# Operands made in two parts between reordered blocks, and right-hand pools moved by 384 bytes

## The chip, the cores and the metric

The kernel runs on one core of a Trainium2 chip. What counts is the time of one execution in device microseconds (us): 597.5 us is the median of three runs of the kernel before.

## The reference

Three stages follow each other on 1152 rows (two batches of 576) of width 512. An attention with random features gives x. A first mixture of experts (MoE 1) sends each row to one of eight experts. A second one (MoE 2) puts every row through all of four experts and adds up the results with weights:

```python
def _moe2_ref(x, domain_probs, w1, w2):
    p = domain_probs / (domain_probs.sum(-1, keepdims=True) + 1e-09)
    out = np.zeros((N, D))
    for e in range(E):                       # 4 experts, D = 512, F = 1024
        h = np.maximum(x @ w1[e], 0.0)
        out += p[:, e:e + 1] * (h @ w2[e])
    return out
```

## The kernel before

Every product is made of three fp32r matmuls (high times high, high times low, low times high; lines 745 to 747). So each operand exists as a pair, a high part that ScalarE casts (line 104) and a low part that VectorE or GpSimd subtracts (line 105); the helper `split` does both.

**MoE 1** works on four chunks of 288 rows, held as columns. For a chunk, `unit1` makes the hidden layer (96 matmuls into `ph`), and `unit2` makes the output in four blocks d = 0 to 3 of 128 features (24 matmuls each into `py`). `add_yt` then multiplies a block by the gate (`yt`, line 826) and adds it to `x2T` (line 828), which has four rows of blocks, [128, 4, 1152]. Chunk c takes the columns 256c to 256c+255 and 32 of the columns above 1024.

**MoE 2** multiplies with a Winograd scheme: seven products instead of eight, of 2x2 blocks. Its columns come in two groups, `GROUPS = ((0, 320), (640, 256))`; group 1 is columns 640 to 1151. `x_side(g)` makes the seven x operands of a group out of `x2T`: high and low parts of the two halves into `xh` and `xl`, a part into `xd`, four sums and differences in place (lines 1111 to 1114), and splits of the results into `xh`, `xl` and, in `rest()`, into `xc`. Group 0 needs chunks 0 to 2, so `x_side(0)` stands ahead of `unit2(3)`. Group 1 needs chunk 3 as well, so `x_side(1)` stands in the main loop, behind the second first-layer step.

The main loop takes two slices (e, j) of the experts' hidden features at a time, an even j (i = 0) and an odd j (i = 1). `layer1(w1, g)` makes seven products `pp` of six matmuls of 320 or 256 columns, in a ring of five PSUM banks that VectorE and ScalarE empty. `layer2` makes a `po` of 512 columns for each of five (g = 0) or four (g = 1) tiles, six matmuls each, in a ring of three PSUM banks; VectorE adds each to `oa` or `ob` (line 1211 for the first slice, line 1213 later). Below, (0,0) is the even slice with group 0, (0,1) the even slice with group 1, and so on. In the first pair the order of the first layers is (0,0), (1,0), (0,1), (1,1); a second layer follows the next first layer.

The order on each engine is made when the program is built: instructions are put in order by their place in the program and by when the scheduler reckons their operands ready; at run time each engine's queue is strictly in order. So `x_side(1)` lies on VectorE between the evictions of the first two `layer1`.

**Addresses.** `w2` of the even slices lies in the pool `w2s0` on the right-hand side of SBUF, that of the odd slices in `w2s1` on the left. The right-hand pools are stacked from the top: `even` (a pad of 32 bytes a partition), `own`, which `xq` (`xd`) replaces later, `xr0` (`xc` of group 0) and `w2s0`. In the program as built before, the four tiles of `w2s0` begin at 201664, 203712, 205760 and 207808, those of `w2s1` at 155200, 157248, 159296 and 161344. Every tile on the left that TensorE reads in the loops here begins 64 bytes past a multiple of 512, those on the right 448 past one. A chunk's columns in `xh` begin 1152 bytes after those of the chunk before. The weights that TensorE loads (`w1` in the first layers, `hh` and `hl` in `layer2`) are all on the left.

Of the kernel before, what the change touches and what calls it, by code (L numbers as in the profile page):

```python
# [9 lines left out]
F32 = mybir.dt.float32  # L10
# [3 lines left out]
ALU = mybir.AluOpType  # L14
# [11 lines left out]
NC = 288  # L26
# [3 lines left out]
GROUPS = ((0, 320), (640, 256))  # L30
# [8 lines left out]
def moe_stack(ctx, tc, q, k, v, omega, w_gate, w_ogate, mw1, mw2, dprobs, dw1, dw2, out):  # L39
    nc = tc.nc  # L40
    TT, STT, TS = nc.vector.tensor_tensor, nc.vector.scalar_tensor_tensor, nc.vector.tensor_scalar

    def f32(ap):
        return ap.bitcast(F32)
# [58 lines left out]
    def split(hi, lo, src, eng=nc.vector, p=lambda i: i):  # L103
        p(nc.scalar.copy(hi, src))  # L104
        p(eng.tensor_tensor(lo, src, f32(hi), op=ALU.subtract))  # L105

    class Expert:
# [45 lines left out]
        def part(self, pool, tag, sink, shape, src, eng=None, p=lambda i: i):  # L153
            hi = pool.tile(shape, F32R, tag=tag + "h", name="whi")
            lo = pool.tile(shape, F32R, tag=tag + "l", name="wlo")
            split(hi, lo, src, eng or self.eng, p)
            sink.append((hi, lo))
# [9 lines left out]
    for c, w, pattern, base in ((0, 32, [[1, 32]], 0), (32, 32, [[1, 32]], 1), (64, 8, [[-1, 8]], 8),  # L167
                                (72, 32, [[0, 4], [1, 8]], 0), (104, 32, [[1, 4], [0, 8]], 0)):
        dst = i32[:, c:c + w]
# [398 lines left out]
    def sel_factors(c, b, eng, p=lambda i: i):  # L568
        t = cp.tile([128, 3, NE], F32, tag="selt", name="selt", bufs=2)
        bc = ohb[:, b:b + 1, :]  # L570
        p(eng.tensor_tensor(t[:, 0:2], g_all[:, 2 * c:2 * c + 2], bc.to_broadcast([128, 2, NE]), op=ALU.mult))
        p(eng.tensor_tensor(t[:, 2:3], grm[:, c:c + 1], bc, op=ALU.mult))

        def total():
            s = cp.tile([128, 3], F32, tag="sel", name="sel", bufs=2)
            p(nc.vector.tensor_reduce(s, t, axis=AX.X, op=ALU.add))
            return s
        return total

    def sel_static(c, b):  # L580
        return sel_factors(c, b, nc.vector)() if b else sel0[c]
# [9 lines left out]
    n = len(units)  # L591
# [19 lines left out]
    def dyn(w, e):  # L611
        return w[bass.ds(e, 1)].rearrange("o a b -> (o a) b")
# [11 lines left out]
    while st < n + 1 or to_turn or to_num or turned:  # L624
# [43 lines left out]
        if 0 <= st - 2 < n and units[st - 2][0] == "q":  # L668
            kind, b, hh, jp = units[st - 2]
# [18 lines left out]
        for x in ready:  # L688
            b, hh, u = x
# [53 lines left out]
    def mm3(ps, st_hl, mv_hl, start, stop):  # L743
        (sh_, sl_), (mh, ml) = st_hl, mv_hl
        nc.tensor.matmul(ps, sh_, mh, start=start, stop=False)  # L745
        nc.tensor.matmul(ps, sh_, ml, start=False, stop=False)  # L746
        nc.tensor.matmul(ps, sl_, mh, start=False, stop=stop)  # L747

    def l1(w1, xhc, xlc, *rings):
        hs = []  # L750
        for f in range(FB):
            pool, tag = rings[f % len(rings)]
            ps = pool.tile([128, NC], F32, tag=tag, name="ph")
            wh, wl = w1[f]
            for kb in range(KB):
                mm3(ps, (wh[:, kb, :], wl[:, kb, :]), (xhc[kb], xlc[kb]), kb == 0, kb == KB - 1)
            if f % 2 == 0:
                hh, hl = h_tiles(NC)
            hid(ps, hh[:, f % 2], hl[:, f % 2])
            hs.append((hh[:, f % 2], hl[:, f % 2]))  # L760
        return hs

    def l2_block(w2, hs, d, bank=None):
        pool, tag = bank or (ps_j, "pj")
        y = pool.tile([128, NC], F32, tag=tag, name="py")
        ds_ = slice(128 * d, 128 * d + 128)
        for f in range(FB):
            wh, wl = w2[f]
            mm3(y, (wh[:, ds_], wl[:, ds_]), hs[f], f == 0, f == FB - 1)
        return y  # L770

    def gate_row(s):

        dg = gp.tile([128, NC], F32, tag="dg", name="dg")
        for t in range(2):
            nc.scalar.activation(dg[:, 128 * t:128 * t + 128], ident, AF.Copy, scale=s[:, t:t + 1])
        nc.scalar.activation(dg[:, 256:NC], fold, AF.Copy, scale=s[:, 2:3])
        ps = nd2.tile([128, NC], F32, tag="nd", name="pg")
        nc.tensor.matmul(ps, ones, dg, start=True, stop=True)
        g = gp.tile([128, NC], F32, tag="gb", name="gb")  # L780
        nc.scalar.copy(g, ps)
        return g
# [3 lines left out]
    def unit1(c, w1, *rings):  # L786
        xhc = [xh[:, kb, NC * c:NC * c + NC] for kb in range(KB)]
        xlc = [xl[:, kb, NC * c:NC * c + NC] for kb in range(KB)]
        return l1(w1, xhc, xlc, *(rings or RINGS))

    def unit2_blocks(c, w2, hs, late=None):
        gb = gate_row(sel_static(c, c // 2))
        for d in range(KB):
            if d == KB - 1 and late is not None:
                late += [l2_block(w2, hs, d, (ps_k, "kv")), gb]
                yield
                return
            y = l2_block(w2, hs, d)
            for dst, src in zip(x2cols(c), (slice(0, 256), slice(256, NC))):
                TT(x2T[:, d, dst], y[:, src], gb[:, src], op=ALU.mult)  # L800
            yield

    def unit2(c, w2, hs):
        if c >= 2:
            gb = gate_row(sel_static(c, c // 2))
            return add_out(w2, hs, gb, list(zip(x2cols(c), (slice(0, 256), slice(256, NC)))))
        for _ in unit2_blocks(c, w2, hs):
            pass

    def x2cols(c):  # L810
        return slice(256 * c, 256 * c + 256), slice(1024 + 32 * c, 1056 + 32 * c)
# [8 lines left out]
    def add_out(w2, hs, gb, cols):  # L820
        for d in range(KB):
            add_yt(l2_block(w2, hs, d), gb, d, cols)

    def add_yt(y, gb, d, cols):
        yt = gp.tile([128, NC], F32, tag="yt", name="yt")
        TT(yt, y, gb, op=ALU.mult)
        for dst, src in cols:
            TT(x2T[:, d, dst], x2T[:, d, dst], yt[:, src], op=ALU.add)

    hs = unit1(0, E0.w1, (ps_j, "pj"), (ps_j, "pj"), (ps_j, "pj"), (ps_k, "kv"))  # L830
# [4 lines left out]
    pool_m = ExitStack()  # L835
    w2p = pool_m.enter_context(tc.tile_pool(name="w2p", bufs=8))
    gp = pool_m.enter_context(tc.tile_pool(name="gp", bufs=2))
    ctx.enter_context(tc.tile_pool(name="even", bufs=1, side="right")).tile([128, 8], F32, name="even")
    pool_o = ExitStack()
    own = pool_o.enter_context(tc.tile_pool(name="own", bufs=1, side="right")).tile([128, KB * 512], F32, name="own")  # L840
    pool_l = ExitStack()
# [1 line left out]
    x2T = yp.tile([128, KB, NX], F32, tag="y", name="x2T")  # L843
# [71 lines left out]
    hs = unit1(1, E0.w1)  # L915
# [57 lines left out]
    E1 = Expert(dyn(mw1, e), None, nc.vector)  # L973
# [48 lines left out]
    with tc.If(nx > 0, preferred_fallthrough_block=True, label="more"):  # L1022
        with tc.For_i(0, nx, 1) as it:
# [7 lines left out]
            hs = l1(E1.w1, xhc, xlc, *RINGS)  # L1031
            Expert(dyn(mw1, ln), None).load1(E1.w1)
            mi = mt[:, bass.ds(it, 1)].rearrange("p o c e -> p (o c) e")
            t = lp.tile([128, 4, 2, NE], F32, tag="xt", name="xt")
# [16 lines left out]
    hs = unit1(2, E1.w1)  # L1051
    unit2(2, E1.w2, hs)
    hs = unit1(3, E1.w1)
# [37 lines left out]
    def pair_of(pool, shape, tags):  # L1091
        return [pool.tile(shape, F32R, tag=t, name=t) for t in tags]

    xa = (xh, xl)
    xd = pair_of(xq, [128, 2, NX // 2], ("xdh", "xdl"))
    xops, xc = [], []

    def x_side(g, eng):
        base, n = GROUPS[g]
        a, b = x2T[:, :, base:base + n], x2T[:, :, base + n:base + 2 * n]  # L1100

        def part(dst, c, src, k=None):
            hi, lo = (t[:, :, c:c + n] for t in dst)
            if k is not None:
                hi, lo, src = (t[:, k:k + 2] for t in (hi, lo, src))
            split(hi, lo, src, eng)
            return [(hi[:, 2 * i:2 * i + 2], lo[:, 2 * i:2 * i + 2]) for i in range(src.shape[1] // 2)]

        b11, b21 = part(xa, base, a)
        b22, = part(xd, base // 2, b[:, 2:4])  # L1110
        eng.tensor_tensor(a[:, 0:2], b[:, 0:2], a[:, 0:2], op=ALU.subtract)
        eng.tensor_tensor(b[:, 0:2], b[:, 2:4], b[:, 0:2], op=ALU.subtract)
        eng.tensor_tensor(b[:, 2:4], b[:, 2:4], a[:, 0:2], op=ALU.subtract)
        eng.tensor_tensor(a[:, 2:4], b[:, 2:4], a[:, 2:4], op=ALU.subtract)
        t1, t4 = part(xa, base + n, a)

        def rest():
            t2, t3 = (part(xc[g], 0, b, i)[0] for i in (2, 0))
            xops.append((b11, b21, b22, t4, t1, t2, t3))

        return rest
# [19 lines left out]
    xc.append(pair_of(xr0, [128, KB, GROUPS[0][1]], ("xch", "xcl")))  # L1141
    x_side(0, nc.vector)()
    w2_ahead = [load_w2(0, 0)]
    unit2(3, E1.w2, hs)
    pool_m.close()
    w2s.append(ctx.enter_context(tc.tile_pool(name="w2s1", bufs=2)))
    xr1 = ctx.enter_context(tc.tile_pool(name="xr1", bufs=1))
# [76 lines left out]
    for p in range(0, 4 * NE2, 2):  # L1224
        ej = [divmod(p + i, 4) for i in range(2)]
        ws = {}
        for i, g in ((0, 0), (1, 0), (0, 1), (1, 1)) if p == 0 else ((0, 0), (0, 1), (1, 0), (1, 1)):
            e, j = ej[i]
            if i not in ws:
                ws[i] = ahead.pop(0) if ahead else load_pair(e, j), w2_ahead.pop() if w2_ahead else load_w2(e, j)  # L1230
            w1, w2 = ws[i]
            h = layer1(w1, g)
            if (p, i, g) == (0, 1, 0):
                x_side(1, nc.vector)()
            if late:
                layer2(*late)
            late = (e, j, g, h, w2)
# [30 lines left out]
```

## Time and profile before

| | |
|---|---|
| runs of the kernel before | 596.45, 597.5, 598.2 us |
| profiled execution: its own time | 597.24 us |
| span of its trace | 595.1 us |
| TensorE busy | 580.5 us (98%) |
| VectorE, ScalarE, GpSimd busy | 397.5, 256.1, 265.3 us |

The span runs from the first instruction to the last; what lies around it, 2.1 us, is start and end of the execution. Times in rows count from the start of the span. A busy TensorE is not one at its best speed: matmuls are pipelined, and a matmul that takes longer looks just as busy.

### The profile page before, as it was taken

Reading aid. Unit: us, or ns where it says so; the run is one execution under the profiler, and the core shown is the slowest. Engines: PE = TensorE matmul, PEld = TensorE weight load, DVE = VectorE, ACT = ScalarE, POOL = GpSimd, SP = SyncE. Lnnn points to the kernel's source line nnn. Section 1 sums busy time; section 2 is a strip of 40 time slices with the busy share of each in tenths; the row PEclk is TensorE's granted clock in tenths of the full one; section 3 lists DMA queues with packets and bytes.
Section 4 is the critical chain, followed back from the end, with each engine's and each line's share of the span. In section 5 each row is a group of like instructions: output and inputs, shape, how many; then the busy total and the mean of one; then the engine's idle time right before and its main releaser. Section 6 shows DMA issues by size and latency. Waiting matters only on the chain.

```text
span 595.1 us, 12003 instructions
## 1 busy us (share of the span) xinstructions
PE 580.5 (98%) x4674; PEld 523.1 (88%) x4675; DVE 397.5 (67%) x889; ACT 256.1 (43%) x625; POOL 265.3 (45%) x316
## 2 busy tenths in 40 slices
PE   9899999999999998999999999999999999999996
PEld 8778788997899997899888988998899889989995
DVE  6688777852667697656766676567566665676564
ACT  5888676023534253343424434334344244333230
POOL 6996085000010033757537456366375473663210
PEclk9999999999999998999999999999999999999999
DMA  7841262154540220022022022022003002200004
GB/s 184 218 124 47 80 208 80 52 215 151 206 145 1 71 72 1 1 72 72 0 72 72 1 72 72 1 72 72 1 20 104 20 1 72 73 0 1 1 0 159
DMA packets 42299, 42.86 MB, mean 72 GB/s; under 512 B 14848, under 2 KB 31488, under 8 KB 42240
## 3 DMA queue, kind: packets, MB, share of 16 engines
q1 hardware_dynamic: 41952, 42.00, 22.2%
q8 instruction: 38, 0.62, 0.4%
q14 instruction: 21, 0.17, 0.1%
q10 hardware_dynamic: 288, 0.07, 0.1%
HBM read 37.34 MB, written 4.72 MB: 71 GB/s over the span
## 4 chain that ended last, share of the span: by engine, by line
PE 67%; DVE 3%; DMA 1%; issue 1%; ACT 0%; SPq 0%; DVEq 0%
PE po L745 11%; PE po L746 11%; PE po L747 11%; PE pp L746 9%; PE pp L745 9%; PE pp L747 9%; PE py L745 1%; DMA st<-in_moe_w_dram 1%; PE py L747 1%; PE py L746 1%; PE ph L747 1%; PE ph L746 1%; PE ph L745 1%; DVE hl L736 1%; DVE c L1174 0%
## 5 line engine op out<-in xcount | busy, mean ns | idle before, releaser
L105 POOL TENSOR_TENSOR wlo<-st,whi 128x512 fp32r<-128x512 f32 x100 | 120.8, 1231 | 188.3 <-ACT whi L104 152.4
L104 ACT CAST whi<-st 128x512 fp32r<-128x512 f32 (+1 forms) x128 | 72.6, 596 | 142.6 <-PE po L747 50.0
L745 PE MATMUL po<-whi,hh 128*128 128x512 f32 x288 | 113.6, 394 | 1.9 <-DVE oa L1211 1.9
L747 PE MATMUL po<-whi,hl 128*128 128x512 f32 x288 | 113.5, 394 | 0.0
L746 PE MATMUL po<-wlo,hh 128*128 128x512 f32 x288 | 113.5, 394 | 0.0
L741 POOL TENSOR_TENSOR hl<-c,hh 128x320 fp32r<-128x320 f32 (+1 forms) x64 | 52.6, 823 | 88.0 <-ACT hh L740 72.3
L747 PE MATMUL pp<-xh,wlo 128*128 128x320 f32 (+1 forms) x256 | 75.8, 296 | 0.0
L746 PE MATMUL pp<-xl,whi 128*128 128x320 f32 (+1 forms) x256 | 75.8, 296 | 0.0
L745 PE MATMUL pp<-xh,whi 128*128 128x320 f32 (+1 forms) x256 | 75.8, 296 | 0.0
L1213 DVE SCALAR_TENSOR_TENSOR oa<-po,pb,oa 128x512 f32<-128x512 f32 x75 | 55.4, 748 | 30.0 <-PE po L747 30.0
L745 PEld LDWEIGHTS po<-whi,hh 128*128 128x128 f32 x288 | 54.3, 188 | 13.0 <-DVE oa L1211 2.1
L747 PEld LDWEIGHTS po<-whi,hl 128*128 128x128 f32 x288 | 54.4, 189 | 12.3
L746 PEld LDWEIGHTS po<-wlo,hh 128*128 128x128 f32 x288 | 54.4, 189 | 10.9
L1213 DVE SCALAR_TENSOR_TENSOR ob<-po,pb,ob 128x512 f32<-128x512 f32 x60 | 44.9, 749 | 28.3 <-PE po L747 28.3
L1174 DVE TENSOR_TENSOR c<-u,pp 128x320 f32<-128x320 f32 (+1 forms) x96 | 43.3, 452 | 22.1 <-PE pp L747 21.7
L739 ACT ACTIVATE c<-c 128x320 f32<-128x320 f32 (+1 forms) x64 | 28.5, 445 | 50.1 <-DVE c L1174 49.1
L745 PEld LDWEIGHTS pp<-xh,whi 128*128 128x128 f32 x256 | 48.6, 190 | 1.4
L746 PEld LDWEIGHTS pp<-xl,whi 128*128 128x128 f32 x256 | 48.6, 190 | 1.3
L747 PEld LDWEIGHTS pp<-xh,wlo 128*128 128x128 f32 x256 | 48.6, 190 | 0.0
L736 DVE SCALAR_TENSOR_TENSOR hl<-c,hh 128x320 fp32r<-128x320 f32 (+1 forms) x64 | 44.5, 729 | 0.2
L339 ACT ACTIVATE e<-pj,nb 128x128 f32<-128x128 f32 x144 | 39.6, 374 | 5.4 <-DVE nb L331 5.0
L745 PE MATMUL py<-hh,whi 128*128 128x288 f32 x128 | 39.3, 307 | 0.0
(263 smaller groups left out, 1272.2 us busy)
## 6 DMA issues: line engine op xcount, KB each, us to landing
st<-in_moe_w_dram SPq DMA_DIRECT2D x36, 512.0 KB, 4.5
st<-in_moe_w_dram SPq DMA_DIRECT2D x9, 1024.0 KB, 5.3
q<-in_q_dram SPq DMA_DIRECT2D x4, 512.0 KB, 5.1
v<-in_v_dram SPq DMA_DIRECT2D x16, 128.0 KB, 4.8
xs<-xn SPq DMA_DIRECT2D x16, 128.0 KB, 2.6
k<-in_k_dram SPq DMA_DIRECT2D x3, 512.0 KB, 4.9
out_dram<-oa SPq DMA_DIRECT2D x5, 256.0 KB, 2.0
own<-in_moe_w_dram SPq DMA_DIRECT2D x1, 1024.0 KB, 6.9
```

Of the source, the lines that this page charges most:

```text
L104: p(nc.scalar.copy(hi, src))
L105: p(eng.tensor_tensor(lo, src, f32(hi), op=ALU.subtract))
L339: pin(nc.scalar.activation(e[:, i], st_p[u][a][:, i], AF.Exp, bias=nb[:, i:i + 1]))
L736: STT(hl, src, 0.0, f32(hh), op0=ALU.max, op1=ALU.subtract)
L739: nc.scalar.activation(c, c, AF.Relu)
L741: nc.gpsimd.tensor_tensor(hl, c, f32(hh), op=ALU.subtract)
L745: nc.tensor.matmul(ps, sh_, mh, start=start, stop=False)
L746: nc.tensor.matmul(ps, sh_, ml, start=False, stop=False)
L747: nc.tensor.matmul(ps, sl_, mh, start=False, stop=stop)
L1174: TT(c, u, p, op=op)
L1213: STT(oacc[T], po, pc, oacc[T], op0=ALU.mult, op1=ALU.add)
```

## The change

It has three parts. The first block order of `unit2(3)` is written out: d = 0, 2, then `x_half(1, 0)`, then d = 1, 3, then `x_half(1, 1)`. Second, `x_half(g, k)` does the part of `x_side(1)` that reads and writes the block rows k and k + 2 of `x2T`; `x_rest` does what was `rest()`, at the place where `x_side(1)` stood. Third, the pad `even` grows from 32 to 416 bytes a partition, so that all right-hand pools lie 384 bytes lower.

```diff
-    ctx.enter_context(tc.tile_pool(name="even", bufs=1, side="right")).tile([128, 8], F32, name="even")
+    ctx.enter_context(tc.tile_pool(name="even", bufs=1, side="right")).tile([128, 104], F32, name="even")
...
+    def x_half(g, k, eng):
+        base, n = GROUPS[g]
+        def quarters(t, c):
+            return t[:, :, c:c + n].rearrange("p (h k) n -> p k h n", k=2)[:, k]
+        def part(dst, c, src):
+            split(*(quarters(t, c) for t in dst), src, eng)
+        a, b = quarters(x2T, base), quarters(x2T, base + n)
+        part(xa, base, a)
+        lo = slice(base // 2, base // 2 + n)
+        split(xd[0][:, k, lo], xd[1][:, k, lo], b[:, 1], eng)
+        eng.tensor_tensor(a[:, 0], b[:, 0], a[:, 0], op=ALU.subtract)
+        eng.tensor_tensor(b[:, 0], b[:, 1], b[:, 0], op=ALU.subtract)
+        eng.tensor_tensor(b[:, 1], b[:, 1], a[:, 0], op=ALU.subtract)
+        eng.tensor_tensor(a[:, 1], b[:, 1], a[:, 1], op=ALU.subtract)
+        part(xa, base + n, a)
+    def x_rest(g, eng):
+        base, n = GROUPS[g]
+        for i in (2, 0):
+            split(xc[g][0][:, i:i + 2], xc[g][1][:, i:i + 2], x2T[:, i:i + 2, base + n:base + 2 * n], eng)
...
-    unit2(3, E1.w2, hs)
+    gb = gate_row(sel_static(3, 1))
+    for k in range(2):
+        for d in (k, k + 2):
+            add_yt(l2_block(E1.w2, hs, d), gb, d, list(zip(x2cols(3), (slice(0, 256), slice(256, NC)))))
+        x_half(1, k, nc.vector)
     pool_m.close()
...
             if (p, i, g) == (0, 1, 0):
-                x_side(1, nc.vector)()
+                x_rest(1, nc.vector)
```

## Rows read from the trace of the kernel before

**Rows 1.** Waits of TensorE: us in total, times, longest us.
```profile
PE po L745 <- DVE oa L1211: 1.9, 1, 1.9
```

**Rows 2.** Windows: us, busy us of each engine, PEclk, DMA share, GB/s.
```profile
200.00:209.00 9.00, 9.00 (x70) 9.00 (x69) 3.75 (x11) 0.56 (x2) 0.00 (x0) 1.00 0.37 117
...
211.00:226.00 15.00, 15.00 (x95) 14.21 (x94) 15.00 (x25) 8.55 (x18) 5.60 (x6) 1.00 0.21 70
...
230.00:232.00 2.00, 2.00 (x6) 1.51 (x6) 0.75 (x1) 0.00 (x0) 0.00 (x0) 0.50 0.00 0
```

**Rows 3.** Timeline of TensorE, 221 to 234 us: start, us, instruction, [idle before].
```profile
221.23 0.39 PE L745 MATMUL po<-whi,hh 128*128 128x512 f32 x1
...
225.40 0.28 PE L745 MATMUL pp<-xh,whi 128*128 128x256 f32 x1
...
226.36 0.28 PE L747 MATMUL pp<-xh,wlo 128*128 128x256 f32 x1
228.55 0.50 PE L745 MATMUL po<-whi,hh 128*128 128x512 f32 x1 [1.92 <-DVE oa L1211]
...
229.82 0.52 PE L747 MATMUL po<-whi,hl 128*128 128x512 f32 x1
...
232.69 0.41 PE L745 MATMUL pp<-xh,whi 128*128 128x256 f32 x1
...
233.33 0.30 PE L745 MATMUL pp<-xch,whi 128*128 128x256 f32 x1
```

**Rows 4.** Timeline of VectorE, 209 to 230 us.
```profile
209.62 1.63 DVE L828 TENSOR_TENSOR x2T<-x2T,yt 128x256 f32<-128x256 f32 x2
...
211.57 1.96 DVE L105 TENSOR_TENSOR xl<-x2T,xh 128x1024 fp32r<-128x1024 f32 x1
...
217.33 1.39 DVE L1112 TENSOR_TENSOR x2T<-x2T 128x512 f32<-128x512 f32 x1
...
223.94 1.21 DVE L105 TENSOR_TENSOR xl<-x2T,xh 128x1024 fp32r<-128x1024 f32 x1
...
226.56 1.28 DVE L105 TENSOR_TENSOR xcl<-x2T,xch 128x512 fp32r<-128x512 f32 x2
227.76 2.05 DVE L1211 TENSOR_SCALAR oa<-po,pb 128x512 f32<-128x512 f32 x3
```

**Rows 5.** Timeline of GpSimd from 200 us on.
```profile
209.88 2.57 POOL L105 TENSOR_TENSOR wlo<-st,whi 128x512 fp32r<-128x512 f32 x2 [33.98 <-issue]
```

**Rows 6.** Windows, tile po alone: four second-layer groups of the second pair.
```profile
271.02:278.02 7.00, 7.00 (x30) 1.00 0.32 121
294.77:301.59 6.82, 6.82 (x30) 1.00 0.01 2
284.17:289.75 5.58, 5.58 (x24) 1.00 0.00 0
307.73:313.21 5.48, 5.48 (x24) 1.00 0.00 0
```

**Rows 7.** Timeline of TensorE, first layers of chunks 0, 1, 2 and 3.
```profile
95.09 0.29 PE L745 MATMUL ph<-xh,whi 128*128 128x288 f32 x1
...
99.96 0.29 PE L746 MATMUL ph<-xl,whi 128*128 128x288 f32 x1
...
116.19 0.29 PE L745 MATMUL ph<-xh,whi 128*128 128x288 f32 x1
...
128.85 0.29 PE L747 MATMUL ph<-xh,wlo 128*128 128x288 f32 x1
...
156.63 0.30 PE L746 MATMUL ph<-xl,whi 128*128 128x288 f32 x1
...
169.02 0.29 PE L747 MATMUL ph<-xh,wlo 128*128 128x288 f32 x1
...
182.86 0.29 PE L745 MATMUL ph<-xh,whi 128*128 128x288 f32 x1
...
195.53 0.29 PE L747 MATMUL ph<-xh,wlo 128*128 128x288 f32 x1
```

More of the change, by code (lines that the diff above doesn't have):

```diff
@@ L1096, in moe_stack, with pair @@
     xops, xc = [], []
+    def x_half(g, k, eng):
[17 more added lines that the diff above has]
+            split(xc[g][0][:, i:i + 2], xc[g][1][:, i:i + 2], x2T[:, i:i + 2, base + n:base + 2 * n], eng)
+        def pair(dst, c, i):
+            return tuple(t[:, i:i + 2, c:c + n] for t in dst)
+        xops.append((pair(xa, base, 0), pair(xa, base, 2), pair(xd, base // 2, 0), pair(xa, base + n, 2),
+                     pair(xa, base + n, 0), pair(xc[g], 0, 2), pair(xc[g], 0, 0)))
     def x_side(g, eng):
```

## Prediction

> **What bounds the kernel now.** I read the waits of TensorE first. In the second mixture only one is left: 1.9 us in which a `po` waits for VectorE's eviction `oa` at line 1211 [rows 1]. The windows around it show why, and what follows. From 211 to 226 us VectorE is busy all the 15 us, so it works off a backlog; from 200 to 209 us, while the last blocks of chunk 3 run, it is busy for 3.75 of 9 us [rows 2]. From 230 to 232 us the granted clock is 0.50, that is 1.2 instead of 2.4 GHz, right behind the wait [rows 2].
>
> The timeline of TensorE gives the price of both. The 18 `po` matmuls from 221.23 to 225.40 us take 0.232 us each, and the eight steps from 225.40 to 226.36 us take 0.12 us each [rows 3]. Between 226.36 and 233.33 us TensorE runs that one step of 0.12, then 12 matmuls of `po` and three of `pp`. At those paces they need 0.12 + 12 x 0.232 + 3 x 0.12 = 3.26 us, so the operation at 233.33 us could have begun at 229.62 us [rows 3]. The place costs 3.7 us: 2.1 us until 228.55 us, 1.6 us of slow matmuls behind it (the slow stretch begins at about 229.82 us and ends at about 233.33 us [rows 3]). From there on TensorE waits for nothing that matters, so what it gains here it keeps until the end.
>
> The last view is the pace of `po` later on. Second pair of slices: 30 matmuls of the even slice take 7.00 us and 30 of the odd one 6.82 us; with group 1 it is 24 in 5.58 against 24 in 5.48 us [rows 6]. The clock is 1.00 in all four and the weights are the same kind of tiles; the pattern repeats in all eight pairs. TensorE is "busy" in both, so only this comparison shows it.
>
> **The change part by part.**
>
> *Work that moves.* In the stretch that VectorE is late in, `x_side(1)` is two subtractions of 1024 columns and five operations of 512 (one subtraction, four sums), and two more subtractions of 512 for `xc`. The prices: 1.21 us for 1024 where nothing is in its way, 1.28 us for two of 512 [rows 4]. So 2 x 1.21 + 5 x 0.64 = 5.6 us, and 1.28 us for `xc`, which stays. A half has two subtractions of 512, one of 256 and four operations of 256. One of 256 costs 0.36 us by the step from 512 to 1024 columns (0.57 us), and less than the 0.64 us of one of 512; I take 0.4 us, near the step. A half is 2 x 0.64 + 5 x 0.4 = 3.3 us on VectorE; two halves are 1 us more than the whole, for seven more instructions. On ScalarE it is three casts more, hidden by its 8.4 idle us of 9 [rows 2].
>
> The first half needs blocks 0 and 2 of chunk 3 and can start when the second block is added, at about 203.8 us. It finds 5.25 idle us on VectorE between 200 and 209 us [rows 2], and GpSimd has nothing to do before 209.88 us [rows 5]. I cost it at nothing. If that cover were gone, it would make the last `add_yt` late, by 3.3 us at most, and the second half with it. As its chain goes from ScalarE to VectorE and back, I expect the last add about 0.4 us later than now. The second half (3.3 us) stays in the late stretch. So the stretch loses 5.6 - 3.3 = 2.3 us of VectorE's work.
>
> There is more to lose: an addition pair that starts at 209.62 us takes 1.63 us, a subtraction of 1024 takes 1.96 instead of 1.21 us, a sum of 512 takes 1.39 instead of 0.64 us [rows 4], and GpSimd is in two subtractions from 209.88 us [rows 5] and in six operations over the stretch [rows 2]. I take these as VectorE held up by GpSimd. With less of VectorE's work there, between 0 and 1.5 us of it (the last two, 0.75 us each) goes too.
>
> *Does the wait go?* The first `oa` starts at 227.76 us and ends about 0.7 us later (2.05 us for three [rows 4]), at 228.4 us. After the change it ends at 228.4 - 2.3 + 0.4 - (0 to 1.5) = 225.0 to 226.5 us. The fourth `po` wants that buffer at 226.48 us if the order on TensorE stays, or at 225.40 us if it comes right behind the third [rows 3]. So the remaining wait is 0 to 1.1 us. I take none, because the order before already puts nine matmuls between them, and the ends that reach 1.1 us need the dearest case twice. Nothing is late next: `xc`, which is first read at 233.33 us now and at 229.6 us without the wait [rows 3], is finished at 227.84 us now [rows 4], so at 228.3 us at the latest. Gain: 3.7 us.
>
> *Waits that are added.* The first cast of each half waits for an `add_yt`. Behind the second one on ScalarE may stand the copy of the first `pp` of the next layer, and behind the sums on VectorE its additions. They free PSUM banks; the ring has five, and TensorE needs the first again five products of six matmuls later, about 4.4 us after it began (six at 0.147 us, an estimate by proportion from 0.12 us for 256 columns and 0.133 us for 288 [rows 3, 7]). A half is 3.3 us, so I cost this at nothing; uncovered it would be the rival "late banks" below. No DMA is issued, moved or passed: the halves run on ScalarE and VectorE alone, and the queues of SP and GpSimd keep their order. The new order of blocks costs TensorE nothing; the matmuls are the same.
>
> *The pad.* All right-hand tiles go from 448 to 64 bytes past a multiple of 512, which is where those on the left are. Does the address matter? A first layer of MoE 1 tests it, all on the left side: `w1` begins 64 bytes past a multiple of 256, a chunk's columns 64 past one for chunks 0 and 2, and 192 past one for chunks 1 and 3. The steps: 4.87 us for 37 in chunk 0 (131.6 ns), 12.66 for 95 in chunk 1 (133.3), 12.39 for 94 in chunk 2 (131.8), 12.67 for 95 in chunk 3 (133.4) [rows 7]. So streamed and loaded operands that lie level modulo 256 go at another pace than those 128 apart, whatever the data. In `layer2` the odd slices' tiles lie level with `hh` and `hl`, the even ones' 128 off, and the even are the slow ones [rows 6]. After the change both are level. So I price even slices at the odd ones' rows: (7.00 - 6.82) + (5.58 - 5.48) = 0.28 us for a pair, 2.2 us for eight. Bounds: 0 if it is not the address, and 2.2 us lost if the new place is as much worse. `xc` and `xd` on the right also change their place. Priced by the 1.7 ns that a matmul of 288 columns differs by, 8 x 2 x (18 + 6) of them are 0.65 us to either side; I take 0, since no row here shows their pace.
>
> The Trainium skill (SBUF — State Buffer, "Who interferes with whom") says that only the port pair that VectorE and GpSimd share causes contention, and that TensorE and ScalarE never wait on anyone. By that the pad could not change a pace, and the sum would lack its 2.2 us. The rows of the first layers above don't agree with its second half, read strictly, but they don't show what is waited for.
>
> **The sum.** Against the profiled execution's own 597.24 us (span 595.1): 597.24 - 3.7 - 2.2 = 591.3 us. The median of the runs is 597.5 us, 0.3 us above that execution, so against the runs the sum is 591.6 us. I say 591.5 us.
>
> **The rivals.**
>
> *The pad does nothing* (0.17). The even slices are slow for another reason, such as where the loop stands when they begin. For it: the same tiles run at 0.232 us in the first group [rows 3] and 0.233 us in the second pair [rows 6], so there is no single pace. Against it: the first layers [rows 7]. Time: 597.24 - 3.7 = 593.5 us. This is also what the skill's rule would give.
>
> *VectorE is still late* (0.15). The scheduler sees VectorE free earlier and puts the fourth `po` close behind the third; 1.1 us of wait stays. If the clock holds, that is 592.4 us; if it falls as before, 1.6 us more, 594.0 us.
>
> *The pad harms* (0.07): the new place is slower for `po` by as much as I hope for. 597.24 - 3.7 + 2.2 = 595.7 us. Nothing in the rows speaks for it, except that only one of several places is known to be good.
>
> *Late banks* (0.08), on the other side. If TensorE's first products of MoE 2, at about 209 us, have to wait for the whole second half, because the strided writes to `xh` and `xl` count as overlapping with what is read, they begin when it ends: 211.3 us (the last add [rows 4]) plus 3.3 us and two casts of about 0.6 us, some 215.8 us. That is 6.8 us of wait, and 1.6 us of clock behind it: 597.24 - 5.9 + 8.4 = 599.7 us. It makes the kernel slower from 5.9 us on, that is if the products begin after about 213.3 us. Against it: the old subtraction into `xl` runs at 211.57 us [rows 4], while TensorE is in products that read other columns of `xl`, so overlap is judged finely.
>
> **How the numbers follow.** The forecast has 0.53: the chance that the wait goes (0.7) and that the pad works (0.75). A measurement of this kernel can tell about 0.3%, 1.8 us; all cases but the last two end below 595.7 us, and the harmful pad at the edge. Faster 0.87, same 0.05, slower 0.08. The range goes from the forecast less 0.65 us for `xc` and `xd` and 0.9 us of the runs' spread (highest run against lowest, 596.45 to 598.2, halved), 589.9 us, up to the dearest of "still late" with the same spread, 595.0 us. That holds the first three cases, 0.85.
>
> **What would show it.** Right: no wait of `po` for `oa`; granted clock 1.00 from 226 to 236 us; the first half's subtractions on VectorE between 204 and 209 us; 30 and 24 `po` of even slices in 6.8 and 5.5 us; first layers of MoE 1 as before. Wrong: a wait of `pp` or `po` near 209 to 216 us; even slices still at 7.0 us; odd ones slower.

## The result, and the profile after

| | before | after |
|---|---|---|
| runs | 596.26 to 598.2 us | 591.41 to 592.21 us |
| median of 4 | 596.98 us | 591.58 us |
| profiled execution: its own time | 597.24 us | 592.21 us |
| its span | 595.1 us | 590.1 us |

The ratio is 0.9909, 95% interval 0.989 to 0.9929. The median fell by 5.4 us, where the sum had 5.9 us; the time is 591.58 us, where 591.5 us was forecast. The range was 589.9 to 595.0 us.

Waits of TensorE, longest in total first (us, times, longest). The wait for `oa` that headed the second mixture [rows 1] is gone; the longest that are left lie in the attention and at the start.

```profile
PE pnd L420 <- DVE xn L409: 1.9, 4, 1.1
PE wu L82 <- DVE ones L76: 1.0, 1, 1.0
```

Windows, as in [rows 2]: the stretch, then busy us of TensorE, its weight loads, VectorE, ScalarE and GpSimd, the granted clock, DMA. VectorE now works 6.62 of the 9 us from 200 on, where it worked 3.75. The late stretch is still nearly full, 14.66 of 15 us. The clock at 230 us is 1.00, and so it is all the way from 226 to 236 us.

```profile
200.00:209.00 9.00, 9.00 (x70) 9.00 (x69) 6.62 (x18) 2.69 (x5) 0.00 (x0) 1.00 0.34 117
211.00:226.00 15.00, 15.00 (x94) 14.23 (x93) 14.66 (x30) 8.15 (x19) 6.33 (x6) 1.00 0.22 70
230.00:232.00 2.00, 2.00 (x19) 2.00 (x18) 1.05 (x3) 1.45 (x4) 1.07 (x1) 1.00 0.04 8
```

TensorE's timeline, first slice pair, second layer of (0,0). All in this trace lies 0.6 us later at the start of MoE 2 (first `pp` at 209.52 instead of 208.93 us). The change does not do that: nearly all of it is there at the first `ph` of MoE 1 (76.53 against 75.98 us), ahead of everything that was changed, and the traces of the experiments have the first `pp` anywhere from 208.75 to 209.69 us. Five `po` stand in a row now, 30 matmuls in 6.82 us; the products that were between the third and the fourth [rows 3] begin behind the fifth. So the program's order on TensorE changed; the forecast had this order only in its rival "VectorE is still late".

```profile
221.90 0.39 PE L745 MATMUL po<-whi,hh 128*128 128x512 f32 x1
...
225.78 0.39 PE L747 MATMUL po<-whi,hl 128*128 128x512 f32 x1
226.00 0.39 PE L745 MATMUL po<-whi,hh 128*128 128x512 f32 x1
...
228.72 0.28 PE L745 MATMUL pp<-xh,whi 128*128 128x256 f32 x1
```

VectorE's timeline. The first half runs from 204.93 to 209.50 us, up to the last subtraction. The last addition pair starts at 210.21 us: with the shift of 0.6 us that is where it was. The first `oa` starts at 224.87 instead of 227.76 us [rows 4] and ends at 225.61 us, 0.4 us before the fourth `po` wants its bank at 226.00 us. The pair of additions (1.63 us) and a subtraction of 256 columns (1.51 us) still show hold-ups.

```profile
204.93 0.69 DVE L105 TENSOR_TENSOR xl<-x2T,xh 128x512 fp32r<-128x512 f32 x1 [0.59 <-ACT xh L104]
...
208.81 0.69 DVE L105 TENSOR_TENSOR xl<-x2T,xh 128x512 fp32r<-128x512 f32 x1 [0.59 <-ACT xh L104]
...
210.21 1.63 DVE L828 TENSOR_TENSOR x2T<-x2T,yt 128x256 f32<-128x256 f32 x2
...
212.37 1.51 DVE L105 TENSOR_TENSOR xdl<-x2T,xdh 128x256 fp32r<-128x256 f32 x1
...
224.87 0.74 DVE L1247 TENSOR_SCALAR oa<-po,pb 128x512 f32<-128x512 f32 x1
```

The `po` of the second pair, even then odd with 30 matmuls, even then odd with 24: the even slices have the odd ones' pace, where it was 7.00 against 6.82 and 5.58 against 5.48 us [rows 6].

```profile
267.73:274.56 6.83, 6.83 (x30) 1.00 0.32 122
291.21:298.04 6.83, 6.83 (x30) 1.00 0.01 2
280.72:286.18 5.46, 5.46 (x24) 1.00 0.00 0
304.20:309.66 5.46, 5.46 (x24) 1.00 0.00 0
```

Two stretches add up the gain. From the first `pp` of MoE 2 to the first `pp` of the second pair the trace had 45.45 us (208.93 to 254.37) and has 41.56 us (209.52 to 251.08). From there to the end of the last `po` it had 336.10 us (to 590.47) and has 334.32 us (to 585.40). That is 3.89 and 1.78 us, less the 0.6 us of the later start: 5.1 us, against 5.0 us by the spans. The first stretch of before holds the fall of the clock.

### The profile page after: what moved, and what is told of

It is laid out like the page before. It is cut to its first block, busy times and chain, and to the rows that moved or that the text cites. A ratio compares the mean times of both kernels' runs of the same rounds, so it can differ in the third digit from the quotient of the medians.

```text
span 590.1 us, 12011 instructions
## 1 busy us (share of the span) xinstructions
PE 577.5 (98%) x4674; PEld 522.8 (89%) x4675; DVE 396.5 (67%) x896; ACT 256.7 (44%) x628; POOL 265.2 (45%) x316
## 4 chain that ended last, share of the span: by engine, by line
PE 70%; DMA 1%; DVE 1%; ACT 0%; issue 0%; SPq 0%; DVEq 0%
PE po L746 11%; PE po L745 11%; PE po L747 11%; PE pp L746 10%; PE pp L747 10%; PE pp L745 10%; DMA st<-in_moe_w_dram 1%; PE py L745 1%; PE py L747 1%; PE py L746 1%; PE ph L747 1%; PE ph L746 1%; PE ph L745 1%; DVE wlo L105 0%; PE pg L779 0%; DVE ob L1249 0%
## 5 line engine op out<-in xcount | busy, mean ns | idle before, releaser
L745 PE MATMUL po<-whi,hh 128*128 128x512 f32 x288 | 112.4, 390 | 0.0
L747 PE MATMUL po<-whi,hl 128*128 128x512 f32 x288 | 112.0, 389 | 0.0
```

## The experiments

Each ratio is to the kernel before, run on the same chip beside it; runs 1 to 4, 5 to 8 and 9 to 12 were on three chips. The clock fell in few executions of the kernel before on the first chip and in nearly all on the second (see "why" below), which moves the ratios by some 0.002. Paces and stretches are read from traces, and of these only that of the kernel before has such a fall ahead of TensorE's last work. "First pair" is the first of the two stretches above, "the other pairs" the second.

**1 and 2: one part of the change each.** Pad alone:

```diff
-    ...side="right")).tile([128, 8], F32, name="even")
+    ...side="right")).tile([128, 104], F32, name="even")
```

> The kernel before with the larger pad alone. Theory (the pace of po depends on where streamed and loaded operands lie to each other modulo 256): even slices take the odd ones' 6.8 and 5.5 us for 30 and 24 matmuls, and the time falls by about 2.2 us, ratio 0.996; the wait of po for oa and the clock of 0.50 behind it stay, 3.7 us. Rival (the even slices are slow because of where the loop stands when they begin, and the halves changed that): even slices stay at 7.0 and 5.6 us, ratio 1.000.

Measured: 594.62 against 596.43 us, ratio 0.9971 (0.9961 to 0.9982); 0.996 was expected. The other pairs take 334.32 us, exactly as after. Windows of `po`, even and odd slice of the second pair:

```profile
269.67:276.50 6.83, 6.83 (x30) 1.00 0.32 118
293.15:299.98 6.83, 6.83 (x30) 1.00 0.01 2
```

The wait of TensorE is still there:

```profile
PE po L745 <- DVE oa L1211: 2.0, 1, 2.0
```

But the clock of the profiled execution is not down behind it (windows as above, TensorE idle for over 1 us in the first):

```profile
226.00:228.00 2.00, 0.88 (x8) 0.68 (x6) 2.00 (x4) 0.37 (x1) 0.20 (x1) 1.00 0.00 0
230.00:232.00 2.00, 2.00 (x12) 1.67 (x11) 0.94 (x3) 0.00 (x0) 0.00 (x0) 1.00 0.00 0
```

So a wait of 2.0 us is not always followed by the clock of 0.50; by the mean clock (0.995 and 0.996) it is in two of this kernel's nine runs. The even slices are fast without the halves: the state of the loop is not what made them slow.

Reordered blocks and halves alone (the kernel after with `tile([128, 8], ...)`):

> The kernel after with the old pad of 32 bytes: reordered blocks and halves alone. Theory (the wait and the slow clock behind it cost 3.7 us and go together): time falls by about 3.7 us, ratio 0.994, no wait of po for oa, clock 1.00 throughout, even slices at 7.0 us for 30 as before. Rival (the wait goes only because po is paced differently, or a shorter wait remains when the pad is old): a wait of up to 1 us stays, and the gain is 1 to 2.6 us, ratio 0.9955 to 0.998.

Measured: 593.93 against 596.43 us, ratio 0.9962 (0.9948 to 0.9975), first pair 41.83 us, the other pairs 336.10 us as before. No wait for `oa`. Against the profiled execution of before the first pair is 3.62 us shorter, as expected; against the runs beside it the gain is 2.3 us, since their clock was mostly up (see "why" below). So the expected ratio of 0.994 was missed, and 0.9962 is in the range that was given to the rival; the rival's sign, a wait that stays, is absent. The even slices are slow as before:

```profile
267.43:274.43 7.00, 7.00 (x30) 1.00 0.33 124
291.17:297.99 6.82, 6.82 (x30) 1.00 0.01 2
```

**3 and 4: other pads.** The kernel after with the right-hand tiles 128 and 256 bytes below their old place:

```diff
-    ...side="right")).tile([128, 104], F32, name="even")
+    ...side="right")).tile([128, 40], F32, name="even")     (3)
+    ...side="right")).tile([128, 72], F32, name="even")     (4)
```

> The kernel after with a pad of 160 bytes in place of 416: right-hand tiles lie 128 bytes lower than before, 320 past a multiple of 512. They are level with the left-hand ones modulo 256, but not modulo 512. Theory (modulo 256 decides): time as after, ratio to before 0.991, even slices at 6.8 us for 30. Rival (modulo 512 decides, or the exact shift): even slices near 7.0 us, ratio 0.994.

Measured: 591.93 against 596.43 us, ratio 0.993 (0.9917 to 0.9944); the other pairs 334.32 us. Even, odd:

```profile
267.30:274.13 6.83, 6.83 (x30) 1.00 0.31 121
290.78:297.61 6.83, 6.83 (x30) 1.00 0.01 2
```

> The kernel after with a pad of 288 bytes: right-hand tiles lie 256 bytes lower than before, 192 past a multiple of 512, so again 128 off modulo 256. Theory (modulo 256 decides): even slices at 7.0 us for 30 matmuls as before, ratio to before 0.994. Rival (any move off the old place helps): even slices at 6.8 us, ratio 0.991.

Measured: 593.71 us, ratio 0.9963 (0.9949 to 0.9976); the other pairs 336.10 us. Even, odd:

```profile
267.46:274.46 7.00, 7.00 (x30) 1.00 0.33 124
291.21:298.03 6.82, 6.82 (x30) 1.00 0.01 2
```

A shift by 128 does all that 384 does, one by 256 does nothing. Modulo 256 decides. Both ratios came out 0.002 nearer to 1 than expected, as in run 2, and run 3's interval alone could not tell theory from rival; the pace of `po` does.

**5: both halves behind the blocks, in the old order of blocks.**

```diff
-    for k in range(2):
-        for d in (k, k + 2):
-            add_yt(l2_block(E1.w2, hs, d), gb, d, ...)
-        x_half(1, k, nc.vector)
+    for d in range(KB):
+        add_yt(l2_block(E1.w2, hs, d), gb, d, ...)
+    for k in range(2):
+        x_half(1, k, nc.vector)
```

> The kernel after, but blocks of chunk 3 in the old order 0, 1, 2, 3 and both halves behind them, so that no half finds VectorE idle. Theory (the gain is the 3.3 us of VectorE's work that moved into idle time): VectorE's stretch after 211 us has both halves, 6.6 us, 1 us more than the old whole, so the wait of po for oa is back at 2 us or more (1 us more for the seven added instructions), and the time is that of the pad alone or up to 1 us longer, ratio to before 0.997 to 0.999. Rival (it is the place in the program, ahead of the first layer of MoE 2, or the smaller pieces that help, not the idle time): no wait of po for oa, ratio 0.993 as with the pad and the reordered blocks.

Measured: 593.08 against 597.33 us, ratio 0.9927 (0.9911 to 0.9944); first pair 43.01 us, 1.45 us longer than after. No wait for `oa`, but two short ones of `pp` for VectorE:

```profile
PE pp L745 <- DVE u L1221: 0.5, 1, 0.5
PE pp L745 <- DVE u L1227: 0.3, 1, 0.3
```

The expectation of a wait at `oa` missed. VectorE's timeline says why: the scheduler begins the first half as soon as its blocks 0 and 2 are there, at 208.17 us instead of 204.93 us, so part of the idle time is still used. The pair of additions of the last block then meets GpSimd and takes 2.73 us:

```profile
208.17 0.69 DVE L105 TENSOR_TENSOR xl<-x2T,xh 128x512 fp32r<-128x512 f32 x1 [0.59 <-ACT xh L104]
...
210.61 2.73 DVE L828 TENSOR_TENSOR x2T<-x2T,yt 128x256 f32<-128x256 f32 x2
```

So this run does not tell idle time from place, as it was meant to; it shows that the new order of blocks is worth 1.45 us of the first pair. Run 11 asks again.

**6: the wait taken away in another way.** The kernel before with the pad, `x_side` whole and where it was:

```diff
-            if e == 0 and j == 0:
+            if e == 0 and j == 0 and g == 0:
+                nc.scalar.activation(oacc[T], po, AF.Copy, scale=pc)
+            elif e == 0 and j == 0:
                 TS(oacc[T], po, pc, None, op0=ALU.mult)
```

> The kernel before with the larger pad, x_side whole and where it was, but the five first evictions of the first slice's group 0 (oa) on ScalarE, which is idle from 227 to 233 us. Theory (what costs time is TensorE's wait for a po bank, not the late operands of group 1): the wait falls from 2.0 us to under 0.5 us, and the first pair of slices takes 41.6 to 42 us as in the kernel after, ratio to before about 0.993. Rival (with the banks free, the next thing is late: xc for the sixth product of group 1, or VectorE's other work): TensorE waits for xc or c instead, 1 us or more, ratio 0.995 to 0.997.

Measured: 591.83 against 597.33 us, ratio 0.9907 (0.9889 to 0.9924); first pair 41.90 us. The list of waits has none for a bank; a short one is left, as the fourth `po` follows the matmul ahead of it after 0.46 instead of 0.23 us. ScalarE evicts the first three from 225.07 us on, 0.6 us each:

```profile
225.07 1.83 ACT L1211 ACTIVATE oa<-po,pb 128x512 f32<-128x512 f32 x3
227.48 0.69 ACT L1211 ACTIVATE oa<-po,pb 128x512 f32<-128x512 f32 x1 [0.59 <-PE po L747]
```

So the price was that of the `po` banks: with these free, nothing of group 1 kept TensorE waiting. These lines do as well as the halves (591.83 us against 591.96 us of run 7 on the same chip, which has the halves).

**7, 8 and 10: absolute and relative place.** All tiles on both sides 64 bytes further up (7), the right-hand ones alone (8), the odd slices' tiles 128 bytes further up (10), each from the kernel after:

```diff
+    cp.tile([128, 16], F32, name="shift")                      (7)
-    ...side="right")).tile([128, 104], F32, name="even")
+    ...side="right")).tile([128, 88], F32, name="even")        (7 and 8)
...
+    ctx.enter_context(tc.tile_pool(name="odd", bufs=1)).tile([128, 32], F32, name="odd")   (10)
     w2s.append(ctx.enter_context(tc.tile_pool(name="w2s1", bufs=2)))
```

> The kernel after with every tile of both sides 64 bytes further up (64 more on the left, a pad of 352 bytes on the right), so that they begin at multiples of 128 and still lie level. Theory (only the places relative to each other count): po, pp and ph at the same pace as after, 30 po in 6.83 us, ratio to before as after, 0.991 to 0.993. Rival (the absolute place counts: the 32 TensorE cycles by which each matmul's step exceeds its columns come from beginning 64 bytes into a line of 128): steps fall towards columns by clock, 30 po in about 6.4 us, and the kernel gains up to 20 us more, ratio 0.96.

Measured: 591.96 us, ratio 0.9908 (0.9891 to 0.9926); the other pairs 334.32 us. Even, odd:

```profile
267.64:274.47 6.83, 6.83 (x30) 1.00 0.30 115
291.12:297.95 6.83, 6.83 (x30) 1.00 0.01 2
```

> The kernel after with the right-hand tiles alone 64 bytes further up (pad of 352 bytes): 64 off the left-hand ones modulo 256. One look at the pace of po for the even slices. Theory (relative place modulo 256, with 0 fast and 128 slow): a value between or equal to one of the two, 6.83 to 7.0 us for 30, and odd slices unchanged at 6.83. Rival (only the remainder modulo 128 counts for speed, and 64 is a place of its own): even slices outside 6.83 to 7.0 us.

Measured in one execution (592.09 us), even and odd:

```profile
267.19:274.07 6.88, 6.88 (x30) 1.00 0.31 117
290.73:297.56 6.83, 6.83 (x30) 1.00 0.01 2
```

> The kernel after with the odd slices' tiles (left-hand side) moved up by 128 bytes, the even ones level. One look at the pace of po. Theory (place relative to the loaded hh and hl modulo 256): odd slices slow, about 7.0 us for 30 and 5.6 for 24, even slices fast at 6.83 and 5.46; span 1.8 us longer than after. Rival (right-hand side or even slices are special): odd slices stay at 6.83.

Measured in one execution (593.39 us): the other pairs 335.87 us, 1.55 us longer than after, where 1.8 us was expected. The pools that follow `w2s1` on the left (`xc` of group 1, VectorE's `u` and `c`, `oa`) moved along; `po` reads none of them. Even, odd:

```profile
267.31:274.14 6.83, 6.83 (x30) 1.00 0.34 127
290.76:297.73 6.97, 6.97 (x30) 1.00 0.01 2
```

Moving both sides by 64 bytes does nothing. It is the distance of the streamed tile from the loaded one, and either side can be the slow one: 30 `po` take 6.83 us at 0, 6.88 us at 64 and 6.97 to 7.00 us at 128 bytes.

**9: a longer wait.** The kernel before, with two more operations on data that nothing reads any more:

```diff
         t1, t4 = part(xa, base + n, a)
+        if g == 1:
+            for _ in range(2):
+                eng.tensor_tensor(a[:, 0:2], a[:, 0:2], a[:, 2:4], op=ALU.subtract)
```

> The kernel before with two more subtractions of 512 columns (1.28 us) on VectorE behind the sums of x_side(1), on data that nothing reads any more. Theory (the wait of po for oa is VectorE's backlog, and the clock of 0.50 follows a wait of about 2 us in some executions and a longer one in more): wait 3.2 us instead of 1.9, the granted clock falls in most executions (mean clock 0.997 or lower), time 1.3 us above before where both fell, ratio 1.002 to 1.005. Rival (the fall has nothing to do with the wait's length): it falls as often as in the runs of before beside it, ratio 1.002.

Measured: 598.59 against 596.38 us, ratio 1.0026 (1.0009 to 1.0044). TensorE waits 2.8 us in all, at two places, where 3.2 us was expected:

```profile
PE po L745 <- DVE oa L1214: 2.0, 1, 2.0
PE pp L746 <- DVE xcl L105: 0.8, 1, 0.8
```

In the profiled execution the clock stays up all the same, also behind the longer wait:

```profile
232.00:234.00 2.00, 2.00 (x10) 1.63 (x9) 1.89 (x4) 0.82 (x2) 0.03 (x1) 1.00 0.00 0
```

Over the runs, the mean granted clock is 0.997 or less in 7 of 12; for the kernel before beside it in 5 of 19. So few executions can't tell these two shares apart, and the rival is not ruled out by the count. What does differ is the depth: five of the 12 have a mean clock of 0.992 to 0.995, where the lowest of those 19 is 0.996. So the longer waits cost more slow clock in some executions; that falls are more frequent is not shown.

**11: x_side(1) whole, behind the blocks in the old order, with the pad.**

```diff
     unit2(3, E1.w2, hs)
+    rest1 = x_side(1, nc.vector)
...
-                x_side(1, nc.vector)()
+                rest1()
```

> The kernel before with the larger pad, and x_side(1) whole right behind unit2(3), blocks in the old order 0 to 3; xc stays where it was. Theory (what helps is work in VectorE's idle time; the place in the program alone only moves VectorE's lateness from the po banks to the pp banks): waits of pp for VectorE between 209 and 222 us, 1 to 3 us in all, first pair of slices 42.5 to 44.5 us against 41.6 after, ratio 0.993 to 0.996. Rival (the two parts are not needed, an earlier place is enough): no such waits, ratio 0.991 as after.

Measured: 594.03 against 596.38 us, ratio 0.9955 (0.994 to 0.997); first pair 43.59 us, 2.0 us longer than after. Waits now at both kinds of banks:

```profile
PE pp L745 <- DVE c L1175: 0.8, 1, 0.8
PE po L745 <- DVE oa L1212: 0.6, 1, 0.6
```

With the same pad as run 1, whose first pair is 43.79 us, the earlier place alone brings 0.2 us. Of the other 2.0 us, 1.45 come with the new order of blocks, which starts the first half 3.2 us earlier (run 5 against after), that is with work in idle time. The remaining 0.6 us lie between the whole (this run) and two halves in the old order (run 5); there smaller pieces and a start in idle time are not told apart.

**12: GpSimd out of the way.** The kernel before; the low parts of `w2` of the first odd slice are left out (zeros).

```diff
+            if (e, j) == (0, 1):
+                nc.scalar.copy(hi, raw_w1[1][:, i, 1])
+                nc.gpsimd.memset(f32(lo), 0.0)
```

> The kernel before, where the low parts of w2 of the first odd slice are left out: GpSimd writes zeros in place of the two subtractions it does from 209.9 us on. One look. Theory (VectorE's operations with two operands in SBUF are held up while GpSimd reads SBUF): the pair of additions at 209.6 us takes about 0.55 instead of 1.63 us and the subtraction of 1024 columns after it 1.2 instead of 1.96 us; VectorE reaches oa 1 to 1.8 us earlier, and the wait of po falls from 1.9 us to between 0 and 0.9. Rival (they wait for ScalarE or for each other): 1.6 and 2.0 us as before, wait 1.9 us.

Measured in one execution (595.26 us), VectorE's timeline:

```profile
209.45 0.53 DVE L828 TENSOR_TENSOR x2T<-x2T,yt 128x256 f32<-128x256 f32 x2
210.78 0.49 DVE L1178 TENSOR_TENSOR c<-s,pp 128x320 f32<-128x320 f32 x1 [0.81 <-PE pp L747]
211.40 1.23 DVE L105 TENSOR_TENSOR xl<-x2T,xh 128x1024 fp32r<-128x1024 f32 x1
...
212.94 1.21 DVE L105 TENSOR_TENSOR xdl<-x2T,xdh 128x512 fp32r<-128x512 f32 x1
...
227.11 2.06 DVE L1215 TENSOR_SCALAR oa<-po,pb 128x512 f32<-128x512 f32 x3
```

GpSimd's:

```profile
209.03 0.99 POOL L1137 MEMSET wlo<- 128x512 f32 x2 [33.34 <-issue]
212.72 0.88 POOL L741 TENSOR_TENSOR hl<-c,hh 128x320 fp32r<-128x320 f32 x1 [2.70 <-ACT hh L740]
```

The wait of TensorE:

```profile
PE po L745 <- DVE oa L1215: 1.4, 1, 1.4
```

The additions take 0.53 instead of 1.63 us [rows 4], while GpSimd only writes, and the subtraction of 1024 columns 1.23 instead of 1.96 us [rows 4], while GpSimd is idle. The next subtraction (512 columns) starts at 212.94 us, behind GpSimd's own, which runs from 212.72 us on, and takes 1.21 us. The wait falls by 0.5 us, not by the 1 us or more expected. The timeline says why: what the additions gain is lost at once, as VectorE then sits idle for 0.81 us until TensorE has the second `pp`, and the subtraction into `xl` begins 0.17 us earlier than before (211.40 against 211.57 us [rows 4]), which is what the whole trace is early by (first `pp` at 208.75 against 208.93 us). What is left is the gain of that subtraction, less the hold-up of the next one.

## Why the prediction was right, point by point

*The wait and its cause: right.* VectorE's backlog held the `po` banks. Moving half of `x_side(1)` (halves alone) and evicting elsewhere (run 6) each take the wait away, all but 0.2 us in run 6, and the first pair is then 41.8 to 41.9 us. The cover was where it was said to be, and the last addition is not late at all, where 0.4 us was reckoned.

*That no wait remains: right, on a thinner margin than it reads.* "The order before already puts nine matmuls between them" failed: the new order puts the fourth `po` right behind the third. It wants its bank at 226.00 us and gets it at 225.61 us. In the old trace's time (0.6 us earlier) the first `oa` ends at 225.0 us, the early end of the forecast's 225.0 to 226.5 us; at the late end 1.1 us of wait would have stayed. So the reason that was given failed, and that the early end came is in part luck. A piece of it is an order that the forecast did not have: before, both `hl` of line 736 stand ahead of the first `oa`; now the second one (0.48 us, at 225.53 us) stands behind it.

*3.7 us for the wait and the clock behind it: right for the profiled execution, too much for most runs.* The first pair of the halves alone is 3.62 us shorter than that of the profiled execution before. But the 1.6 us of slow clock are not paid in every run. The mean clock tells the runs apart, roughly: in the profile before, with the fall behind the wait, it is 0.997; a fall in the last microseconds alone leaves 0.998 or more in the profiles here. In the 33 runs of kernels whose `po` does not wait for `oa` (after, runs 2 to 8 and 10; 0.2 us in run 6) it is never below 0.998, so the lower values go with the wait. Of 38 runs of the kernel before beside these experiments (two far off the rest left out), it is 0.997 or less in 2 of 12, 6 of 7 and 5 of 19. In the last set, those five have a median of 597.65 us, the other 14 of 596.15 us: 1.5 us, which is the term's size. So the change gains 4.2 us where few runs of before pay it (by the ratio of run 3, 0.993) and 5.5 us where nearly all do (run 7, 0.9908). The step that was mis-sized is "Gain: 3.7 us" as a gain of every run; it is 2.1 us and, in some, 1.6 us more. That 591.3 us was so near does not speak for 3.7 us as the gain: the sum takes the price of the fall from an execution that had paid it, so the time after comes out right whether other executions pay it or not.

*2.2 us for the pad: right.* Halves alone against the kernel after: 336.10 - 334.32 = 1.78 us in the other pairs and 41.83 - 41.56 = 0.27 us in the first, 2.05 us together; pad alone 1.7 us by its ratio. Modulo 256 was read from four first layers of another stage, 288 columns wide; runs 3, 4, 7, 8 and 10 bear it out for `po`. For the first layers themselves it stays a reading: they go at 131.5, 133.3, 131.8 and 133.3 ns before and after, and no run moved their operands against each other. The bound of 0.65 us for `xc` and `xd` to either side was not used, though these tiles went from 128 off to level as well, so the sentence on "streamed and loaded operands" is too wide, as 320 and 256 columns show no such difference: `pp` groups of 42 take 6.15 to 6.16 and 5.02 to 5.03 us in both traces (254.37 to 260.52 against 251.08 to 257.24 us, and 266.00 to 271.02 against 262.70 to 267.73 us).

*VectorE held up by GpSimd: shown by run 12* for two operations, 1.1 and 0.7 us. How much of it the change took away is not shown.

*The rivals.* "The pad does nothing" and "the pad harms" fell with runs 1 and 3. "VectorE is still late" was half right: the fourth `po` did move right behind the third, but its bank was free. "Late banks" did not come: runs 5 and 11 have waits of `pp` of 0.8 us, but for VectorE's own work, not for falsely overlapping writes. What in TensorE makes a distance of 128 bytes slow stays open; only that it does was tried. Nor is the distance all: 24 `po` of the odd slices went from 5.48 [rows 6] to 5.46 us, though their own operands lie level in both kernels.

The Trainium skill (SBUF — State Buffer, "Who interferes with whom") puts all contention at the port pair of VectorE and GpSimd and says that TensorE never waits on anyone. Run 12 agrees with its first half, that a two-operand VectorE instruction is held up by a GpSimd instruction that reads SBUF (1.63 against 0.53 us). Runs 3, 4 and 10 do not fit the second half as the prediction used it, that a place in SBUF cannot change TensorE's pace: 30 `po` take 6.83 or 7.00 us by where TensorE's own two operands lie. What TensorE waits for there they do not show.

## What to carry to other kernels

Compare the pace of matmuls that should be alike: two groups of the same shape at 227 and 233 ns, in a trace that calls both busy, were worth 2 us here and cost a pad of some bytes. When an engine is late, look for idle time of that engine earlier on, and for the smallest piece of its late work whose operands are there by then; or for one late instruction that an idle engine can do, which took two lines here and did as well (run 6). A price read from one profiled execution can hold a part, such as a fall of the clock, that other executions don't pay: look at the mean clock of all the runs before putting it into a sum.

## What was not expected of the hardware

- The granted clock of 0.50 (1.2 GHz) came behind a TensorE wait of 1.9 us in one execution and not behind 2.0 us in another; by the mean clock, which does not show the place of a fall, it came in 13 of 38 runs of the kernel before, and in none of 33 runs of kernels without that wait.
- The step of a 512-column matmul, 30 in a row, rises with the distance of its two operands modulo 256 bytes: 227.6 ns at 0, 229.3 ns at 64, 232.3 to 233.3 ns at 128. For 320 and 256 columns the groups' times changed by no more than 0.01 us.
- Three `po` evictions took 1.83 us on ScalarE and 2.05 us on VectorE [rows 4].
